# Three quotients of a fused attention and Mish kernel: from a logarithm and an exponential on ScalarE to a power of -1 on GpSimd

## The chip, the core and the metric

The kernel runs on one core of a Trainium2 chip. The core has five engines that run at the same time, each with its own queue of instructions that it works off in order: TensorE (PE in the profile; its weight loads are listed apart as PEld), VectorE (DVE), ScalarE (ACT), GpSimd (POOL) and SyncE (SP), which here only issues transfers. The metric is the device time of one execution in microseconds. Three runs of the kernel before took 1613.51, 1614.98 and 1616.91 us; the median is 1614.98 us.

## What is computed

The input x has 2048 rows of 512 numbers. Its normalized rows go two ways: through an attention of 32 heads of width 16 that share one key and one value head, and through two dense layers with a Mish activation between them. The output is x plus the product of the attention's result and a gate.

```python
xn = _layernorm(x)                                   # 2048 x 512
q = xn @ wq ; k = xn @ wk ; v = xn @ wv              # 32 heads of q, one of k and of v, width 16
p = _softmax(q k^T * 16 ** -0.5)                     # 32 x 2048 x 2048
s = (p @ v) @ wo                                     # 2048 x 512
h = xn @ w1 + b1                                     # 2048 x 1792
act = h * tanh(softplus(h))                          # Mish
y = act @ w2                                         # 2048 x 512
out = x + s * (y * sigmoid(y))
```

Three quotients are in it. With t = exp(h), tanh(softplus(h)) is t(t + 2) / (t(t + 2) + 2): the quotient of the first layer. The sigmoid of y is 1 / (1 + exp(-y)): the gate. And the attention divides each head's sum of p times v by the sum of its exponentials: the softmax.

## The kernel before, in words

All tiles have 128 partitions and, mostly, 512 columns of float32. The rows of x form four chunks of 512 (c = 0 to 3). Products that need full precision are made of three matmuls on numbers split into a high and a low part, so that most weights and activations exist as a pair of tiles ("high" by a copy to a rounded type, `hi_pool`; "low" by a subtraction, `sub`).

The work is written out by a Python program that decides the order of every instruction while it builds the kernel; the chip then only follows that order, with semaphores where one engine needs another's result. Order and waits are fixed; if an engine is later than the planner thought, the others wait for it.

- A **lead** of some 95 us normalizes x, makes keys and values and starts the first work. It has a planner of its own with a duration for each task; where TensorE has nothing to do it is given "warm" matmuls (L1178), whose results nobody reads.
- Then come 512 **steps** (the loop over `s`, L1286), 16 for each of 32 units of one head group. In a step TensorE makes four score tiles `e` (L875), ScalarE turns each into `pt` by an exponential (L877), and TensorE multiplies the `pt` of two steps ago by the values (`pv`, L949, the last matmuls of a step). TensorE also makes four tiles `m` (L895) for units to come; VectorE takes their row maxima (`mb`, L899), which give the shifts of the exponentials. `e` has three buffers in PSUM and `m` three.
- Between these matmuls lie the **dense matmuls** (`xps`), taken from a queue of groups of 12 or 15: the query groups (`q_group`), the first layer (`m1_group`, 14 per chunk, one for every 128 of the 1792 columns), the second layer (`m2_groups`, three thirds of 5, 5 and 4 first-layer tiles, four groups each) and the output projection (`wo_groups`). A group takes four steps: its matmuls are cut into chunks of 6 (or 8 and 7), and each chunk is done by halves of the partitions in two steps. A group is taken up only when the planner believes that its inputs are ready and the buffers that it will need free. If none is, the step has no dense matmuls. After step 490 no `m` are left, and a step has four dense matmuls over all partitions.
- What follows a group is a chain over other engines. **First layer** (`post` in `m1_group`, L647): ScalarE adds the bias (`hb`, L652); a "job" on ScalarE makes t = exp(hb) (L658); GpSimd limits it (L163), makes u = t + 2 (L661), u = u t and hb = hb u (L153); two more jobs on ScalarE make t = ln(u + 2) (L667) and t = exp(-t) (L671); then GpSimd multiplies hb by t and splits it into the pair `act` (L148, L153), which the second layer reads. **Gate** (L726 to L743): exp(-y) on ScalarE (L729), limited on GpSimd, ln(e + 1) and exp(-e) on ScalarE (L734, L739), y times e on GpSimd; four per chunk. **Softmax** (L972 to L990): once per 128 columns of heads, ln and exp(-) of the sums `sc` on ScalarE (L973, L977), then on GpSimd the product with `oc` and the split into `ot_all`, which the output projection reads.

Jobs are small pieces for ScalarE that wait in a list; `act_jobs` (L349) places one of them behind the exponentials of a step, two if more than two wait, and none in a step that had to move a result out of PSUM unless more than two wait. On GpSimd the planner keeps a clock: `charge(us)` (L133) adds the duration that it assumes for an operation (0.7 for one input, 1.3 for two), and `pool_at` (L143) gives the step at which the engine will be through, at 2.95 us per step. The first layer has three `hb` buffers, and the `t` tiles (which the gate shares) two.

The last unit's attention is finished by `o_last` (L1001), which has its own short form with a logarithm and an exponential; the change leaves it alone.

Of the kernel before, what the change touches and what calls it, by code (L numbers as in the profile page):

```python
# [14 lines left out]
F32 = mybir.dt.float32  # L15
F32R = mybir.dt.float32r
AF = mybir.ActivationFunctionType
ALU = mybir.AluOpType
AX = mybir.AxisListType

P = 128
# [26 lines left out]
NACT = 7  # L48
AHEAD = 2
THIRDS = ((0, 5), (5, 10), (10, 14))  # L50
TMAX = 2.0 ** 14
EMAX = 2.0 ** 60
TERMS = ((0, 0), (0, 1), (1, 0))
# [62 lines left out]
def block_kernel(ctx: ExitStack, tc: tile.TileContext, x, wq, wk, wv, wo, w1, b1, w2, out):  # L116
    nc = tc.nc
    cp = ctx.enter_context(tc.tile_pool(name="const", bufs=1))
# [8 lines left out]
    pe, act, dve, pool, sp = nc.tensor, nc.scalar, nc.vector, nc.gpsimd, nc.sync  # L127
# [5 lines left out]
    def charge(us):  # L133
        busy[0] = max(busy[0], step[0] * STEP_US + (0 if lead else 1.5)) + us
# [8 lines left out]
    def pool_at(margin):  # L143
        return max(math.ceil(2 * (busy[0] / STEP_US + margin)) / 2, step[0])
# [16 lines left out]
    def pool_min(o, lim):  # L161
        charge(0.7)
        pool.tensor_scalar(o, o, lim, 0.0, op0=ALU.min, op1=ALU.max)  # L163

    def f(ap):
        return ap.bitcast(F32)

# [1 line left out]
    dve.memset(f(qts[0]), 0.0)  # L169
    ident = cp.tile([P, P], F32, name="ident")  # L170
    make_identity(nc, ident)
    two = cp.tile([P, 1], F32, name="two")
    dve.memset(two, 2.0)
    one = cp.tile([P, 1], F32, name="one")
    dve.memset(one, 1.0)
    wk3 = sb.tile([P, 2, NDT, 64], F32R, tag="oc", name="wk3", bufs=1)
    wkf = sb.tile([P, NDT, 64], F32, tag="os", name="wkf", bufs=1)
    ks = cp.tile([P, S], F32R, name="ks")
# [144 lines left out]
    for j in range(4):  # L323
        o = slice(DH * j, DH * (j + 1))
# [6 lines left out]
    def at(s, fn):  # L331
        if s <= step[0]:
            fn()
        else:
            timed.setdefault(s, []).append(fn)

    def later(k, fn):
        at(step[0] + k, fn)
# [3 lines left out]
    def job(fn, free=None):  # L342

        jobs.append((fn, free))
# [299 lines left out]
    def m1_group(c, ft):  # L644
        it = item("ws", ("1", ft), w1[:, P * ft:P * (ft + 1)].rearrange("(t p) n -> p t n", p=P))

        def post(ps):  # L647
            hb = sb.tile([P, C], F32, tag="hb", name=f"hb{c}_{ft}", bufs=NHB)
            free_hb = hold(hb_hist)
            st = {}  # L650
            bias = b1c[:, ft:ft + 1]
            act.activation(hb, ps, AF.Identity, bias=bias)  # L652
            gap[0] += 1
            def st1():
                t = st["t"] = sb.tile([P, C], F32, tag="t", name=f"t{c}_{ft}", bufs=2)
                u = st["u"] = sb.tile([P, C], F32, tag="u", name=f"u{c}_{ft}", bufs=2)
                st["free"] = hold(t_hist)
                act.activation(t, hb, AF.Exp)  # L658
                pool_min(t, TMAX)
                charge(0.7)  # L660
                pool.tensor_scalar(u, t, 2.0, 1.0, op0=ALU.add, op1=ALU.mult)  # L661
                mul(pool, u, u, t)
                at(pool_at(0.3), lambda: job(st2))
                mul(pool, hb, hb, u)

            def st2():
                act.activation(st["t"], st["u"], AF.Ln, bias=two)  # L667
                job(st3)

            def st3():  # L670
                act.activation(st["t"], st["t"], AF.Exp, scale=-1.0)  # L671
                later(0.5, st4)

            job(st1, t_free)

            def st4():
                if extra(c, ft) == 0:
                    a = sb.tile([P, 2, C], F32R, tag="wq", name=f"act{c}_{ft}", bufs=1)
                elif extra(c, ft) == 1:
                    a = qts[(NU - 3) % 3]  # L680
                else:
                    a = sb.tile([P, 2, C], F32R, tag="act", name=f"act{c}_{ft}", bufs=NACT)
                act_of[c, ft] = a
                mul(pool, hb, hb, st["t"])
                st["free"]()
                hi_pool(a[:, 0], hb)
                sub(pool, a[:, 1], hb, f(a[:, 0]))
                m1_done[c, ft] = pool_at(0.2)
                free_hb()

        def slot():
            if extra(c, ft) >= 0:
                return 16 * (NU - 2) * extra(c, ft)
            return act_free[0] if act_live[0] < NACT else None

        def start():
            act_live[0] += extra(c, ft) < 0

        g = Group(mm12(lambda j, a: it.tile[:, a, P * j:P * (j + 1)],
                       lambda j, b_: xt_of[c][:, b_, j], NDT), post, [it],  # L700
                  [lambda: hb_hist[-NHB], slot, lambda: xt_done.get(c)], start=start)
        g.m1 = ft
        return g

    def m2_groups(c, third, its, m1s):
        lo, hi = THIRDS[third]

        def ready():
            return m1_done.get((c, hi - 1))

        def mk(tt):
            def post(ps):
                if tt == 3:
                    act_live[0] -= hi - lo
                if third == 0:
                    y_of[tt] = sb.tile([P, D], F32, tag=f"y{tt}", name=f"y{c}_{tt}", bufs=1)
                    act.activation(y_of[tt], ps, AF.Copy)
                    gap[0] += 1
                    return
                y = y_of[tt]  # L720
                dve.tensor_tensor(out=y, in0=ps, in1=y, op=ALU.add)  # L721
                if third < 2:
                    return
                st = {}

                def s1():  # L726
                    e = st["e"] = sb.tile([P, D], F32, tag="t", name=f"e{c}_{tt}", bufs=2)
                    st["free"] = hold(t_hist)
                    act.activation(e, y, AF.Exp, scale=-1.0)  # L729
                    pool_min(e, EMAX)  # L730
                    at(pool_at(0.3), lambda: job(s2))

                def s2():
                    act.activation(st["e"], st["e"], AF.Ln, bias=one)  # L734
                    job(s3)

                def s3():
                    e = st["e"]
                    act.activation(e, e, AF.Exp, scale=-1.0)  # L739
                    mul(pool, y, y, e)  # L740
                    y_done[c, tt] = pool_at(0.2)
                    st["free"]()
                later(0.5, lambda: job(s1, t_free))  # L743

            g = Group(mm12(lambda j, a: act_of[c, lo + j][:, a, P * tt:P * (tt + 1)],
                           lambda j, b: its[j].tile[:, b], hi - lo), post, its, [ready])
            g.dve = third > 0
            return g
        return [mk(tt) for tt in range(4)]
# [201 lines left out]
    def o_out(v):  # L951
        c, g = divmod(v, 8)
        b, k = divmod(g, 2)
        os_ = sb.tile([P, C], F32, tag="os", name=f"os{v}", bufs=1)
        if v == NU - 1:
            o_last(os_)
            return
        act.activation(os_, pv_of[v], AF.Copy)
        if k == 0:
            o_of[0] = sb.tile([P, C], F32, tag="oc", name=f"oc{v}", bufs=1)  # L960
            o_of[1] = sb.tile([P, C], F32, tag="sc", name=f"sc{v}", bufs=1)
        oc, sc = o_of[0], o_of[1]
        for e, t in ((16, sc), (0, oc)):
            for j in range(4):
                r = 64 * k + 16 * j
                sp_at(0.63)
                sp.dma_start(t[r:r + 16], os_[32 * j + e:32 * j + e + 16])
        rows = slice(0, HALF if v == NU - 2 else P)
        if v == NU - 2:
            turn_rows()  # L970
        if k == 1 or v == NU - 2:
            def n0():  # L972
                act.activation(sc[rows], sc[rows], AF.Ln)  # L973
                job(n1)

            def n1():
                act.activation(sc[rows], sc[rows], AF.Exp, scale=-1.0)  # L977
                later(0.5, n2)

            def n2():  # L980
                if b == 0 and c > 0 and wo_left[c - 1]:
                    later(0.5, n2)
                    return
                ot = ot_of[c, b] = ot_all[:, b]
                mul(pool, oc[rows], oc[rows], sc[rows])
                hi_pool(ot[rows, 0], oc[rows])
                sub(pool, ot[rows, 1], oc[rows], f(ot[rows, 0]))
                if k == 1:
                    ot_done[c, b] = pool_at(0.2)
            later(3, lambda: job(n0))  # L990

    turn_of = {}

# [120 lines left out]
    st = [task("DVE", 0.83, lambda t=t: stats(t), at=xat[t], prio=t // 4 * 2) for t in range(16)]  # L1114
    kv_done = None
    for c0, c1 in ((0, 1), (1, 2), (2, 4)):
# [4 lines left out]
        for c in range(c0, c1):  # L1121
            xs, his = [], []
            for t in range(4 * c, 4 * c + 4):
                sc = task(*(("ACT", 0.72), ("DVE", 0.4))[c == 0], lambda t=t: x_scale(t), [nrm])
# [72 lines left out]
    rows = []  # L1197
    cdone = [None]
    kind = [None]
    while True:  # L1200
# [21 lines left out]
        s, e, k = min(opts, key=lambda o: o[0])  # L1222
# [129 lines left out]
```

## Time and profile before

| | |
|---|---|
| runs, median (lowest to highest) | 1614.98 us (1613.51 to 1616.91) |
| span of the profiled execution | 1612.9 us |
| PE busy | 1594.2 us, 99% |
| DVE busy | 1348.5 us, 84% |
| ACT busy | 1294.7 us, 80% |
| POOL busy | 620.8 us, 38% |
| granted TensorE clock, mean | 0.999 |

The profile is of one execution. Its span runs from the first to the last instruction; the runs' times are of whole executions, and the one that was profiled has no time of its own beside the span. The span lies 2.1 us below the median of the runs, which is less than the 3.4 us between the lowest and the highest of them. A row of instructions gives line, engine, operation, what it writes and reads with the shape, and the count; then the busy time, the mean of one in ns, and the idle time of the engine just before these instructions, with what ended it. A row of a stretch gives its limits in us from the span's start, its length, then for each engine the busy time and the number of instructions, and at the end the granted clock and the transfers' share. A row of the waits gives who waited for whom, the total in us, how often, and the longest.

### The profile page before, as it was taken

What the parts mean: (1) busy time and instruction counts of PE and PEld (TensorE: products, weight loads), DVE (VectorE), ACT (ScalarE), POOL (GpSimd) and SP (SyncE); (2) the same over time, 40 slices, a digit from 0 to 9 for tenths busy, and PEclk for the clock granted to TensorE, in tenths of its full rate; (3) what the DMA queues carried; (4) which work ended last, traced back from release to release, by engine and by line L of the source; (5) the groups of instructions that cost most, each with busy time, mean ns of one, the idle gap of its engine ahead of it and who ended that gap; (6) DMA issues with size and microseconds to landing.
All of it is one profiled execution on the core that took longest, in us unless ns stands there. A gap on an engine that the chain in (4) does not pass through costs nothing.

```text
span 1612.9 us, 31471 instructions
## 1 busy us (share of the span) xinstructions
PE 1594.2 (99%) x11615; PEld 851.9 (53%) x11615; DVE 1348.5 (84%) x2300; ACT 1294.7 (80%) x2490; POOL 620.8 (38%) x627
## 2 busy tenths in 40 slices
PE   8999999999999999999999999999999999999998
PEld 5455545555555555555555555555555555555534
DVE  8988888888988888888898988888889898888802
ACT  5478788788888778877988787797788878879885
POOL 3875176166265103421524133154153223315522
PEclk9999999999999999999999999999999999999999
DMA  5332133042231304212113321231241313022020
GB/s 161 145 115 64 41 122 111 15 148 83 70 114 52 109 23 153 70 31 91 52 27 111 92 75 26 91 119 38 67 135 34 113 57 96 23 73 78 21 86 26
DMA packets 72776, 127.30 MB, mean 79 GB/s; under 512 B 21488, under 2 KB 34288, under 8 KB 72112
## 3 DMA queue, kind: packets, MB, share of 16 engines
q1 hardware_dynamic: 72624, 125.30, 24.9%
q8 instruction: 92, 1.51, 0.4%
q14 instruction: 60, 0.49, 0.1%
HBM read 76.36 MB, written 27.26 MB: 64 GB/s over the span
## 4 chain that ended last, share of the span: by engine, by line
PE 95%; DVE 2%; ACT 1%; DMA 1%; issue 0%; POOL 0%; SPq 0%; DVEq 0%; ACTq 0%; POOLq 0%
PE xps L109 46%; PE pv L949 31%; PE m L895 8%; PE e L875 5%; PE xps L105 3%; DVE mb L899 1%; PE wop L105 1%; PE warm L1178 0%; PE kp L289 0%; ACT xin L194 0%; DMA xin<-in_dram 0%; DVE st L214 0%; DMA ws<-w 0%; DVE xin L240 0%; PE xp L250 0%
## 5 line engine op out<-in xcount | busy, mean ns | idle before, releaser
L899 DVE TENSOR_REDUCE mb<-m 128x1 f32<-128x512 f32 x2048 | 1272.8, 683 | 184.4 <-PE m L895 157.5
L877 ACT ACTIVATE pt<-e 128x512 f32<-128x512 f32 x2048 | 1068.4, 604 | 253.0 <-PE e L875 236.8
L895 PE MATMUL m<-ks,qt 48*128 48x512 f32 (+1 forms) x2048 | 837.4, 422 | 3.0 <-DVE mb L899 2.5
L875 PE MATMUL e<-qt,ks 64*128 64x512 f32 x2048 | 746.4, 410 | 0.0
L949 PE MATMUL pv<-pt,vaug 128*32 128x512 f32 x4096 | 545.3, 605 | 0.0
L895 PEld LDWEIGHTS m<-ks,qt 48*128 48x128 f32 (+1 forms) x2048 | 370.6, 185 | 67.2 <-DVE mb L899 35.2
L875 PEld LDWEIGHTS e<-qt,ks 64*128 64x128 f32 x2048 | 370.7, 186 | 26.3 <-ACT pt L877 19.6
L109 PE MATMUL xps<-xt,ws 64*128 64x512 f32 x1248 | 345.8, 410 | 0.4 <-POOL ws L153 0.2
L109 PEld LDWEIGHTS xps<-xt,ws 64*128 64x128 f32 x1248 | 215.2, 185 | 205.9 <-ACT pt L877 135.2
L109 PE MATMUL xps<-wbs,act 64*128 64x512 f32 x1158 | 312.9, 407 | 0.1
L109 PEld LDWEIGHTS xps<-wbs,act 64*128 64x128 f32 x1158 | 201.9, 185 | 166.8 <-ACT pt L877 101.5
L949 PEld LDWEIGHTS pv<-pt,vaug 128*32 128x32 f32 x4096 | 80.7, 108 | 141.9 <-issue 133.2
L163 POOL TENSOR_SCALAR t<-t 128x512 f32<-128x512 f32 x56 | 34.5, 616 | 278.4 <-ACT t L658 278.4
L153 POOL TENSOR_TENSOR hb<-hb,t 128x512 f32<-128x512 f32 x56 | 72.3, 1292 | 152.4 <-PE m L895 74.0
L109 PE MATMUL xps<-xt,wq 64*128 64x512 f32 x336 | 93.0, 409 | 0.0
L109 PEld LDWEIGHTS xps<-xt,wq 64*128 64x128 f32 x336 | 58.0, 185 | 55.4 <-ACT pt L877 35.2
L109 PE MATMUL xps<-wbs,ot_all 64*128 64x512 f32 x288 | 79.3, 407 | 0.0
L109 PEld LDWEIGHTS xps<-wbs,ot_all 64*128 64x128 f32 x288 | 49.5, 184 | 47.2 <-ACT pt L877 30.2
L153 POOL TENSOR_TENSOR hb<-hb,u 128x512 f32<-128x512 f32 x56 | 72.3, 1291 | 4.4
L153 POOL TENSOR_TENSOR u<-u,t 128x512 f32<-128x512 f32 x56 | 71.9, 1284 | 4.7
L153 POOL TENSOR_TENSOR act<-hb,act 128x512 fp32r<-128x512 f32 x55 | 70.9, 1289 | 4.6
L721 DVE TENSOR_TENSOR y<-xps,y 128x512 f32<-128x512 f32 x32 | 21.9, 683 | 58.0 <-PE xps L105 58.0
(116 smaller groups left out, 826.7 us busy)
## 6 DMA issues: line engine op xcount, KB each, us to landing
ws<-w SPq DMA_DIRECT2D x38, 512.0 KB
wbs<-w SPq DMA_DIRECT2D x36, 512.0 KB
qt<-qh SPq DMA_DIRECT2D x256, 32.0 KB
w<-ws SPq DMA_DIRECT2D x14, 512.0 KB
w<-wbs SPq DMA_DIRECT2D x14, 512.0 KB
wq<-wq SPq DMA_DIRECT2D x13, 512.0 KB
wbs<-wo SPq DMA_DIRECT2D x12, 512.0 KB
rawwb<-in_dram SPq DMA_DIRECT2D x20, 256.0 KB
```

Of the source, the lines that this page charges most:

```text
L105: self.pe.matmul(ps, self.lhs(), self.rhs(), start=(self.k == 0), stop=(self.k == self.tot - 1))
L109: i = self.pe.matmul(ps, self.lhs()[o], self.rhs()[o], start=(self.k == 0 and self.halves == 0), stop=(self.k == self.tot - 1 and self.hal ...
L153: eng.tensor_tensor(out=o, in0=a, in1=b, op=op)
L163: pool.tensor_scalar(o, o, lim, 0.0, op0=ALU.min, op1=ALU.max)
L721: dve.tensor_tensor(out=y, in0=ps, in1=y, op=ALU.add)
L875: pe.matmul(e, ks[o:o + 64, P * k:P * (k + 1)], q[o:o + 64, p], start=True, stop=True)
L877: r = act.activation(pt, e, AF.Exp, scale=0.25)
L895: pe.matmul(m, q[o, p, P * t:P * (t + 1)], ks[o, C * kb:C * (kb + 1)], start=True, stop=True)
L899: return dve.reduce_max(out=mb_of[v][:, kb, z:z + 1], in_=m, axis=AX.X)
L949: pe.matmul(o[32 * j:32 * j + 32], vaug[:, k], pt, start=(k == 0), stop=(k == 15))
```

## The change

A new helper `inverse` raises a tile to the power of -1 on GpSimd, by an operation on two tiles whose second input is a column of -1 repeated along the row; if asked, it first adds a constant with an operation of its own. The planner is told 4.0 us for the power (`POW_US`). The first layer calls it with u + 2, the gate with e + 1, the softmax with `sc` alone. The logarithms and exponentials that did this on ScalarE go, and with them the jobs and the waits in planned steps between the engines: after the first exponential the rest of each chain is issued to GpSimd in one piece.

```diff
+POW_US = 4.0
...
+    def inverse(o, i, add=None):
+        if add is not None:
+            charge(0.7)
+            pool.tensor_scalar(i, i, add, 1.0, op0=ALU.add, op1=ALU.mult)
+        charge(POW_US)
+        pool.tensor_tensor(out=o, in0=i, in1=minus[0:i.shape[0]].to_broadcast(list(i.shape)), op=ALU.pow)
+
...
-    two = cp.tile([P, 1], F32, name="two")
-    dve.memset(two, 2.0)
-    one = cp.tile([P, 1], F32, name="one")
-    dve.memset(one, 1.0)
+    minus = cp.tile([P, 1], F32, name="minus")
+    dve.memset(minus, -1.0)
...
                 mul(pool, u, u, t)
-                at(pool_at(0.3), lambda: job(st2))
                 mul(pool, hb, hb, u)
-
-            def st2():
-                act.activation(st["t"], st["u"], AF.Ln, bias=two)
-                job(st3)
-
-            def st3():
-                act.activation(st["t"], st["t"], AF.Exp, scale=-1.0)
-                later(0.5, st4)
+                inverse(t, u, 2.0)
+                st4()
...
                     pool_min(e, EMAX)
-                    at(pool_at(0.3), lambda: job(s2))
-
-                def s2():
-                    act.activation(st["e"], st["e"], AF.Ln, bias=one)
-                    job(s3)
-
-                def s3():
-                    e = st["e"]
-                    act.activation(e, e, AF.Exp, scale=-1.0)
+                    inverse(e, e, 1.0)
                     mul(pool, y, y, e)
...
             def n0():
-                act.activation(sc[rows], sc[rows], AF.Ln)
-                job(n1)
-
-            def n1():
-                act.activation(sc[rows], sc[rows], AF.Exp, scale=-1.0)
-                later(0.5, n2)
+                inverse(sc[rows], sc[rows])
+                n2()
...
-            later(3, lambda: job(n0))
+            later(3, n0)
```

## The prediction

> **What bounds the kernel now.** I read the page's shares first, then the chain that ended last, then the waits, then stretches of the step loop.
>
> ```profile
> PE 1594.2 (99%) x11615; PEld 851.9 (53%) x11615; DVE 1348.5 (84%) x2300; ACT 1294.7 (80%) x2490; POOL 620.8 (38%) x627
> PE 95%; DVE 2%; ACT 1%; DMA 1%; issue 0%; POOL 0%; SPq 0%; DVEq 0%; ACTq 0%; POOLq 0%
> ```
>
> The second line is the chain by engine: TensorE carries 95% of it, ScalarE, which the change relieves, 1%, and GpSimd, which it loads, 0%. Who waits says the same:
>
> ```profile
> ACT pt L877 <- PE e L875: 236.8, 439, 1.1
> DVE mb L899 <- PE m L895: 157.5, 375, 1.2
> PEld e L875 <- ACT pt L877: 19.6, 33, 0.8
> ```
>
> ScalarE waits 236.8 us for scores and VectorE 157.5 us for `m`; the other way, score weights wait for an exponential 33 times, 19.6 us, and weight loads overlap matmuls. So ScalarE has slack in most steps already. Stretches of the loop show what sets a step:
>
> ```profile
> 901.56:936.45 34.89, 34.89 (x265) 18.96 (x264) 31.41 (x55) 25.28 (x51) 4.49 (x4) 1.00 0.30 91
> 1252.09:1275.27 23.18, 23.18 (x179) 12.53 (x177) 20.81 (x37) 19.93 (x39) 1.91 (x2) 1.00 0.35 114
> 446.67:469.66 22.99, 22.99 (x178) 12.39 (x177) 20.47 (x38) 20.87 (x42) 17.77 (x18) 1.00 0.28 98
> 224.25:232.37 8.12, 7.32 (x51) 2.68 (x49) 7.34 (x13) 6.83 (x15) 7.50 (x9) 1.00 0.50 163
> 232.37:235.52 3.15, 3.15 (x25) 1.51 (x23) 2.69 (x6) 2.77 (x6) 2.98 (x4) 1.00 0.98 349
> 58.00:82.00 24.00, 22.99 (x94) 12.48 (x93) 23.86 (x41) 8.49 (x15) 19.56 (x20) 1.00 0.36 122
> 96.89:1527.40 1430.51, 1427.52 (x10817) 767.40 (x10816) 1247.52 (x2106) 1185.59 (x2282) 536.28 (x538) 1.00 0.25 77
> ```
>
> The first three are whole steps with a dense chunk of 6: 12, 8 and 8 of them, so 2.908, 2.897 and 2.874 us each. ScalarE's count above four per step is its other work: 3, 7 and 10 instructions, and more of it makes no step longer. The fourth is three steps without dense matmuls, 2.71 us each; the fifth is the step behind them, 3.15 us. The sixth lies in the lead, where VectorE is full; the last is the loop while `m` lasts.
>
> **The change part by part.** Removed from ScalarE:
>
> ```profile
> L667 ACT ACTIVATE t<-u,two 128x512 f32<-128x512 f32 x56 | 41.6, 743 | 2.2 <-POOL u L153 2.2
> L671 ACT ACTIVATE t<-t 128x512 f32<-128x512 f32 x56 | 36.5, 651 | 0.1
> L734 ACT ACTIVATE e<-e,one 128x512 f32<-128x512 f32 x16 | 11.9, 742 | 0.8 <-POOL e L163 0.8
> L739 ACT ACTIVATE e<-e 128x512 f32<-128x512 f32 x16 | 10.4, 652 | 0.1
> L977 ACT ACTIVATE sc<-sc 128x512 f32<-128x512 f32 (+1 forms) x16 | 10.5, 659 | 0.0
> L973 ACT ACTIVATE sc<-sc 128x512 f32<-128x512 f32 (+1 forms) x16 | 10.4, 653 | 0.0
> ```
>
> These are 176 instructions and 121.3 us, 9% of ScalarE's busy time. Almost all lies beside TensorE. Directly it can give back no more than the 19.6 us of weight waits, and the matmuls behind them lost far less; nearest to zero, I take -1.5 us, bounds 0 and -20.
>
> Against it stands what the quiet steps show: the first stretch has 0.25 other ScalarE instructions a step, the second 0.9, and the step with fewer is 0.011 us longer, so 0.016 us per job, +2.9 us for 176. GpSimd's load works the other way: with about as many jobs a step, its busy share is 8% in the second stretch and 77% in the third, and the step is 0.023 us shorter, 0.03 us per full share. Nothing explains either, so I hold them for correlations. At 4 us a power GpSimd's share rises by a quarter (below): over the 364 six-matmul steps -3 us. I let the two cancel and keep ±3.
>
> Added to GpSimd: 88 powers (56, 16, 16), 72 additions (0.62 us by the row of L661 below), and by the order of the built kernel three high parts from ScalarE. The rows of a first-layer block:
>
> ```profile
> L163 POOL TENSOR_SCALAR t<-t 128x512 f32<-128x512 f32 x56 | 34.5, 616 | 278.4 <-ACT t L658 278.4
> L661 POOL TENSOR_SCALAR u<-t 128x512 f32<-128x512 f32 x56 | 34.8, 621 | 4.6
> L153 POOL TENSOR_TENSOR u<-u,t 128x512 f32<-128x512 f32 x56 | 71.9, 1284 | 4.7
> L153 POOL TENSOR_TENSOR hb<-hb,t 128x512 f32<-128x512 f32 x56 | 72.3, 1292 | 152.4 <-PE m L895 74.0
> L148 POOL TENSOR_SCALAR act<-hb 128x512 fp32r<-128x512 f32 x55 | 34.2, 622 | 4.8
> L153 POOL TENSOR_TENSOR xt<-xf,xt 128x1024 fp32r<-128x1024 f32 x2 | 4.8, 2382 | 3.0 <-ACT xt L274 3.0
> ```
>
> No row shows the power, P. Below it cannot be cheaper than a two-input operation of its size, 1.29 us. Above, no row bounds it; I take 8 us, six such passes, because a power needs a logarithm and an exponential. I take 4.0, the planner's charge, because the charges that have rows stand within 14% above them (0.7 for 0.62, 1.3 for 1.29, 2.5 for 2.38); likely P is 3.5 to 4.0. That this charge was measured too is my assumption.
>
> GpSimd's total at 4.0: 620.8 + 88 x 4.0 + 75 x 0.62 = 1019 us, 63%. The total fits; the question is local. A block has four operations of 0.62, four of 1.29 and the power; with some 0.07 us between starts (66.47 and 67.17 below for an operation of 0.62) it takes 8.3 + P, 12.3 us at 4.0. A first-layer group is four steps, 11.5 us. So GpSimd becomes the slower partner in runs of first-layer groups. The planner knows: it charges 12.0 per block and takes groups up accordingly, but at 2.95 us per step; at the measured 2.88 its 12.0 us pass in 11.7, so GpSimd falls behind by 0.6 us a block, 3 us over the five of a third. That is hidden, because the fourth and fifth tile of a third are read only two steps, 5.8 us, after its first group begins. Cost 0 at P = 4.0; with that cover gone the lateness lands on TensorE.
>
> In the built order the loop's steps without dense matmuls go from 12 in 9 places to 7 in 5, nearly all in the first chunk, and 18 dense matmuls leave the lead for the loop. Five filled steps cost 5 x (2.88 - 2.71) = +0.9; four fewer catch-up steps give 4 x (3.15 - 2.88) = -1.1. In the lead, warm matmuls replace the 18; VectorE is full there (23.86 of 24.00), so its end stays: 0, bounds ±1.
>
> SP's transfers keep their kind, and one is added; the query copies issued by SP stay at their planned steps, but their source on GpSimd comes later:
>
> ```profile
> 58.91 0.60 POOL L163 TENSOR_SCALAR t<-t 128x512 f32<-128x512 f32 x1
> ...
> 66.47 0.62 POOL L163 TENSOR_SCALAR t<-t 128x512 f32<-128x512 f32 x1
> 67.17 0.62 POOL L661 TENSOR_SCALAR u<-t 128x512 f32<-128x512 f32 x1
> ...
> 72.03 1.29 POOL L153 TENSOR_TENSOR ql<-qf,qh 128x512 fp32r<-128x512 f32 x1
> ```
>
> Two blocks with powers ahead of it put `ql`, done at 73.3, near 85 us; its copies are placed behind the loop's first steps, after 92 us. Behind them in SP's queue stand weight loads: 0 at P = 4.0.
>
> The end of the kernel, where the last two gates stand:
>
> ```profile
> 1589.05 0.65 ACT L729 ACTIVATE e<-y 128x512 f32<-128x512 f32 x1
> 1605.49 1.28 POOL L153 TENSOR_TENSOR xr<-xr,y 128x512 f32<-128x512 f32 x1 [5.64 <-DVE y L153]
> 1607.25 1.28 DVE L153 TENSOR_TENSOR y<-wop,y 128x512 f32<-128x512 f32 x2
> ```
>
> After 1589.70 GpSimd does two chains of limit, addition, power and product, 2 x (2.8 + P): at 4.0 until 1603.3. The next GpSimd work is due at 1605.49 and VectorE reads the last gate after 1607.25: hidden by 2.2 us, until P = 5.1, from where each us costs two.
>
> Sum against the span: -1.5 + 0 + 0.9 - 1.1 = -1.7, so 1611.2 us; the median of the runs lies 2.1 above the span, so 1613.3 us; I say 1613.5.
>
> **Rivals.** First, slower: the power takes longer than 4.0. Lateness per third is 5 x (8.3 + P - 11.7), against 5.8 us of cover, so it decides from P = 4.6, and in the first chunk, where weight splits fill GpSimd too, from about 4.2. With 12 thirds, P = 5 costs 12 x 2.2 = 26 us (1640), P = 5.5 some 56 (1670), P = 8 over 200. This is an upper count, since weight reloads and two blocks ahead soften it; I would halve it: 1627, 1642 and above 1715. For it: nothing measured shows P. Against: the charges' closeness to the rows.
>
> Second, faster: the step's dependence on GpSimd's share is real (-3 us), the one on jobs is not (0), and ScalarE's crowding costs a quarter of the 19.6 us of weight waits (-5). With the -0.2 of the empty steps that is 8.2 below the median, 1607 us. For it speaks the third stretch; against it that the first, with the least other work on ScalarE, is the slowest of the three.
>
> Third, a delay D at the first use of the power, in the lead. GpSimd's first block begins at 58.91; three blocks of 12.3, the query split and the weight split that the loop's first dense group needs (1.9 each) end near 99.6. It is read near 100.6, an empty step (2.7) and a step's `pv` (1.0) after 96.9. So the delay costs D - 1.0 once. The rows show no such gap before other first uses on GpSimd. For D = 3 it is +2, 1615 us. The Trainium skill's GPSIMD Engine Reference, section 2.1 "Instruction dispatch", says that the first call into freshly loaded GpSimd code pays about 6 us that no instruction shows; by that page, an estimate, it would be +5 us, 1618. No run here shows it for this operation.
>
> That the change does less than it says is no rival: the ScalarE instructions are gone from the built order.
>
> **Chances.** No change of weight, P at most 4.2: 0.52 (1609 to 1618; of it faster 0.14, same 0.26, slower 0.12). Power too slow: 0.30, slower. Faster rival: 0.14. First use: 0.04, same or slower by halves. About 0.2%, 3.2 us, is what a measurement of this kernel can tell. Together faster 0.28, same 0.28, slower 0.44. The range goes down to 1606 for the second rival and up to 1650, P near 6 by the halved count.
>
> **What would show it.** The power's row gives P: at most 4.2 for the forecast. ACT busy near 1175 us, POOL near 1020, ScalarE's wait for scores up, no new row of weight loads waiting for GpSimd's `act` or `ws`. Wrong if P is over 4.6, if ScalarE's exponentials wait for GpSimd to free `t` or `hb`, or if the last gate ends after 1605.

## The result: five times slower

The changed kernel takes 8076.66 us (median; 8074.56 to 8077.45), the kernel before 1614.6 us on the same chip: 5.0001 times as long, interval 4.9938 to 5.0064. The forecast was 1613.5 us with a range up to 1650. From the page of the kernel after, its first lines and the chain that ended last, by engine:

```profile
span 8072.6 us, 31665 instructions
PE 1782.0 (22%) x11639; PEld 920.5 (11%) x11639; DVE 1363.0 (17%) x2299; ACT 1207.6 (15%) x2311; POOL 7862.2 (97%) x784
POOL 60%; issue 5%; PE 1%; SPq 0%; DMA 0%; POOLq 0%; ACT 0%; DVE 0%; ACTq 0%
```

TensorE has gone from 99% of the span to 22%, and GpSimd from 38% to 97%; of the chain that ended last, GpSimd carries 60% of the span and TensorE 1%. One line of the kernel makes nearly all of GpSimd's time (groups of GpSimd, each shape by itself):

```profile
L171 POOL TENSOR_TENSOR t<-u,minus 128x512 f32<-128x512 f32 x56 | 4588.2, 81932 | 4.7
L171 POOL TENSOR_TENSOR e<-e,minus 128x512 f32<-128x512 f32 x16 | 1310.9, 81930 | 1.3
L171 POOL TENSOR_TENSOR sc<-sc,minus 128x512 f32<-128x512 f32 x15 | 1228.8, 81922 | 38.0 <-DMA sc<-os 38.0
L171 POOL TENSOR_TENSOR sc<-sc,minus 64x512 f32<-64x512 f32 x1 | 81.9, 81915 | 0.0
```

One power takes 81.93 us, not 4.0. The 88 of them take 4588.2 + 1310.9 + 1228.8 + 81.9 = 7209.8 us; GpSimd's other work is 7862.2 - 7209.8 = 652 us, and it stands idle for 210 us. These three make the span. Shared out over the powers, the loss is (8076.66 - 1614.6) / 88 = 73.4 us for each; if all of it is theirs, only 8.5 us of each is hidden.

The timeline of GpSimd around the first power (start, length, line) shows a whole block:

```profile
60.96 0.62 POOL L164 TENSOR_SCALAR t<-t 128x512 f32<-128x512 f32 x1
...
65.09 0.62 POOL L169 TENSOR_SCALAR u<-u 128x512 f32<-128x512 f32 x1
65.79 81.94 POOL L171 TENSOR_TENSOR t<-u,minus 128x512 f32<-128x512 f32 x1
147.81 1.26 POOL L154 TENSOR_TENSOR hb<-hb,t 128x512 f32<-128x512 f32 x1
...
151.10 0.62 POOL L164 TENSOR_SCALAR t<-t 128x512 f32<-128x512 f32 x1
```

From one block's first operation to the next it is 151.10 - 60.96 = 90.14 us, that is 8.2 + P: the prediction's block of 8.3 + P, with another P. How the other engines come to stand still is read from the waits (who for whom, total, times, longest):

```profile
DVE mb L890 <- PE m L886: 5625.4, 462, 174.9
PEld e L866 <- ACT pt L868: 3312.3, 58, 161.6
ACT t L664 <- POOL hb L154: 1921.9, 23, 162.3
PE m L886 <- DMA qt<-ql: 798.5, 10, 149.2
ACT e L728 <- POOL y L154: 741.1, 8, 156.4
PE xps L110 <- POOL ws L149: 621.3, 6, 174.3
```

Read from the cause upward: ScalarE's next job needs a `t` tile that GpSimd has not freed, 1921.9 us in 23 waits for the first layer and 741.1 in 8 for the gate, up to two powers at a time. Behind that job in ScalarE's queue stand the exponentials of the scores, so TensorE's score weights wait for `pt`, and VectorE waits for TensorE. The query's low parts and the weight splits, which stand in GpSimd's own queue behind powers, stop TensorE directly. The waits overlap and are not to be added up. Two stretches, one of the loop and one in it:

```profile
96.89:1527.40 1430.51, 341.40 (x2316) 176.23 (x2316) 272.61 (x453) 242.82 (x463) 1384.95 (x196) 0.61 0.06 21
98.00:156.00 58.00, 5.73 (x21) 3.23 (x25) 4.47 (x8) 6.89 (x13) 57.33 (x10) 0.50 0.00 0
```

In the time in which the kernel before did nearly its whole loop, TensorE worked 341 us, at a mean granted clock of 0.61; while it stands still behind a power, the clock is 0.50. The Trainium skill's "TensorE: Matmul & The Clock Gate", Part 1, says that the clock falls to half when TensorE has been idle for a window of some 3.4 us; the second row agrees.

At the end the last four gates run one behind another with nothing beside them (GpSimd's timeline):

```profile
7728.63 81.93 POOL L171 TENSOR_TENSOR e<-e,minus 128x512 f32<-128x512 f32 x1
7813.38 81.93 POOL L171 TENSOR_TENSOR e<-e,minus 128x512 f32<-128x512 f32 x1
7898.13 81.93 POOL L171 TENSOR_TENSOR e<-e,minus 128x512 f32<-128x512 f32 x1
7982.88 81.93 POOL L171 TENSOR_TENSOR e<-e,minus 128x512 f32<-128x512 f32 x1
```

### The profile page after: what moved, and what is told of

The parts are those of the page before. It is cut to its first block, busy times and chain, and to the rows that moved or that the text cites. A ratio compares the mean times of both kernels' runs of the same rounds, so it can differ in the third digit from the quotient of the medians.

```text
span 8072.6 us, 31665 instructions
## 1 busy us (share of the span) xinstructions
PE 1782.0 (22%) x11639; PEld 920.5 (11%) x11639; DVE 1363.0 (17%) x2299; ACT 1207.6 (15%) x2311; POOL 7862.2 (97%) x784
## 4 chain that ended last, share of the span: by engine, by line
POOL 60%; issue 5%; PE 1%; SPq 0%; DMA 0%; POOLq 0%; ACT 0%; DVE 0%; ACTq 0%
POOL t L171 37%; POOL e L171 12%; POOL sc L171 7%; POOL hb L154 1%; POOL u L154 1%; POOL act L154 0%; POOL u L169 0%; POOL u L667 0%; SPq L958 0%; POOL t L164 0%; POOL act L149 0%; PE xps L110 0%; PE pv L940 0%; POOL oc L154 0%; POOL ot_all L154 0%
## 5 line engine op out<-in xcount | busy, mean ns | idle before, releaser
L171 POOL TENSOR_TENSOR t<-u,minus 128x512 f32<-128x512 f32 x56 | 4588.2, 81932 | 4.7
L866 PE MATMUL e<-qt,ks 64*128 64x512 f32 x2048 | 812.9, 442 | 3849.7 <-ACT pt L868 3282.7
L171 POOL TENSOR_TENSOR sc<-sc,minus 128x512 f32<-128x512 f32 (+1 forms) x16 | 1310.8, 81922 | 38.0 <-DMA sc<-os 38.0
L171 POOL TENSOR_TENSOR e<-e,minus 128x512 f32<-128x512 f32 x16 | 1310.9, 81930 | 1.3
L886 PE MATMUL m<-ks,qt 48*128 48x512 f32 (+1 forms) x2048 | 897.3, 452 | 800.7 <-DMA qt<-ql 798.5
L866 PEld LDWEIGHTS e<-qt,ks 64*128 64x128 f32 x2048 | 409.9, 205 | 3898.8 <-ACT pt L868 3312.3
L110 PE MATMUL xps<-xt,ws 64*128 64x512 f32 x1272 | 393.8, 445 | 1017.1 <-POOL ws L149 621.3
L940 PE MATMUL pv<-pt,vaug 128*32 128x512 f32 x4096 | 599.3, 660 | 0.0
L886 PEld LDWEIGHTS m<-ks,qt 48*128 48x128 f32 (+1 forms) x2048 | 403.5, 201 | 867.5 <-issue 803.5
L664 ACT ACTIVATE t<-hb 128x512 f32<-128x512 f32 x56 | 36.0, 643 | 2291.9 <-POOL hb L154 1921.9
L728 ACT ACTIVATE e<-y 128x512 f32<-128x512 f32 x16 | 10.1, 632 | 1272.2 <-POOL y L154 741.1
```

The source lines that it names most:

```text
L110: i = self.pe.matmul(ps, self.lhs()[o], self.rhs()[o], start=(self.k == 0 and self.halves == 0), stop=(self.k == self.tot - 1 and self.hal ...
L171: pool.tensor_tensor(out=o, in0=i, in1=minus[0:i.shape[0]].to_broadcast(list(i.shape)), op=ALU.pow)
L866: pe.matmul(e, ks[o:o + 64, P * k:P * (k + 1)], q[o:o + 64, p], start=True, stop=True)
L886: pe.matmul(m, q[o, p, P * t:P * (t + 1)], ks[o, C * kb:C * (kb + 1)], start=True, stop=True)
L940: pe.matmul(o[32 * j:32 * j + 32], vaug[:, k], pt, start=(k == 0), stop=(k == 15))
```

## The experiments

The theory after the result: the length of the power on one in-order engine explains the loss, and nothing else in the change does. Rivals: the form of the operation (the repeated column, the tile's shape, the exponent) makes it slow; or the new order and the waits cost much by themselves. Beside these stood a smaller question: what would the change have done with the power at the price that the prediction took?

**The price by itself.** Six powers and one reciprocal are added behind the kernel before:

```diff
+    power(P, 512, pm.to_broadcast([P, 512]))
+    power(P, 256, pm.to_broadcast([P, 256]))
+    power(P, 64, pm.to_broadcast([P, 64]))
+    power(16, 512, pm[0:16].to_broadcast([16, 512]))
+    power(P, 512, p2)
+    power(P, 512, ph.to_broadcast([P, 512]))
+    dve.reciprocal(pd, p1)
```

Here `pm` is a column of -1 (`pminus` in the profile), `p2` a full tile of -1 (`pexp`) and `ph` a column of 2 (`phalf`).

> The kernel before, with six powers on GpSimd behind its last work, on a tile of 2.5: 512, 256 and 64 columns with a repeated column of -1; 512 columns on 16 partitions; 512 columns with a full tile of -1; 512 columns with an exponent of 2. They only lengthen the end. Theory: the power costs 0.160 us per column, whatever the partitions, the exponent and the way the second input is laid out: 82, 41, 10, 82, 82 and 82 us, and the span is 1613 + 379 = 1992 us. Rival 1, the repeated column is what is slow: the fifth takes 1.3 to 4 us and the span is near 1912 us. Rival 2, the exponent of -1 (a reciprocal) is slow: the sixth takes a few us.

Measured 1993.2 us against 1614.9. The groups:

```profile
L1353 POOL TENSOR_TENSOR pout<-pin,pexp 128x512 f32<-128x512 f32 x1 | 82.1, 82142 | 0.1
L1353 POOL TENSOR_TENSOR pout<-pin,pminus 128x512 f32<-128x512 f32 x1 | 81.9, 81948 | 1.7 <-DVE phalf L1350 1.7
L1353 POOL TENSOR_TENSOR pout<-pin,phalf 128x512 f32<-128x512 f32 x1 | 81.9, 81917 | 0.1
L1353 POOL TENSOR_TENSOR pout<-pin,pminus 16x512 f32<-16x512 f32 x1 | 81.9, 81905 | 0.1
L1353 POOL TENSOR_TENSOR pout<-pin,pminus 128x256 f32<-128x256 f32 x1 | 41.1, 41120 | 0.1
L1353 POOL TENSOR_TENSOR pout<-pin,pminus 128x64 f32<-128x64 f32 x1 | 10.5, 10515 | 0.1
L1360 DVE RECIPROCAL dout<-pin 128x512 f32<-128x512 f32 x1 | 3.3, 3343 | 0.0
```

The price goes by columns: (41.120 - 10.515) / 192 = 0.159 us per column and 0.3 us once. A full tile of exponents, an exponent of 2, or 16 rows in place of 128 change it by at most 0.3%. The rival of the form falls: no choice among these made the power cheap. An operation on one tile with the exponent as a constant was not run. The Trainium skill's "GPSIMD Engine Reference", section 2, says that each of GpSimd's eight cores has 16 partitions of its own; that 16 rows cost what 128 do agrees with it.

**One quotient at a time.** The kernel before with the power in the gate alone (the 16 quotients of L734 and L739 become `inverse(e, e, 1.0)`, as in the change), and with the power in the softmax alone (the 16 of L973 and L977).

> The kernel before with the power in the gate alone: 16 powers, the first layer and the softmax keep their logarithm and exponential. Theory (GpSimd works its queue in order, and everything behind a power waits for it, so that nearly the whole of each power shows): in the kernel after, each of 88 powers cost (8076.7 - 1614.6) / 88 = 73.4 us of the kernel's time; 16 x 73.4 = 1175, so 2790 us, and the last four gates alone, one behind another after the loop, cost 4 x 82 = 328 us. Rival (GpSimd stands idle for 62% of the kernel before, 992 us, and that absorbs most of the 16 x 81.9 = 1311 us that only four tiles per chunk wait for): GpSimd's total becomes 621 + 1311 + 10 = 1942 us and bounds the kernel, so at most some 1960 us.

> The kernel before with the power in the softmax alone: 16 powers, spread evenly, one every 32 steps (92 us). Theory (nearly the whole of each power shows, since the first layer's work stands behind it in GpSimd's queue and the shifts and products of the loop wait for that): 1615 + 16 x 73.4 = 2790 us. Rival (spread evenly, a power of 82 us fits into the idle 62% of its 92 us, less the 35 us that GpSimd works in it: 25 us late per power): 1615 + 16 x 25 = 2015 us, GpSimd nearly full.

Measured 2790.7 and 2622.1 us against 1616.8: 73.4 us per power of the gate, 62.8 per power of the softmax. The theory gave 2790 for both: the gate met it, the softmax came out 168 us below it. That the gate's 73.4 is also the mean over the 88 is in part luck, since four of its 16 powers run at the end with nothing beside them. GpSimd has 30% and 26% of the spans to spare, and still most of each power shows. Who waits, first in the run with the gate, then in the run with the softmax:

```profile
PEld e L877 <- ACT pt L879: 785.5, 42, 82.6
ACT e L739 <- POOL y L154: 555.2, 8, 84.1
```

```profile
PEld e L885 <- ACT pt L887: 859.0, 40, 75.5
ACT t L677 <- POOL u L154: 387.0, 13, 72.7
ACT t L668 <- POOL hb L154: 342.0, 6, 68.2
```

It is the chain read above. The softmax's powers, spread evenly over the loop, stop it too, because the first layer's products stand behind them in GpSimd's queue and ScalarE's queue waits for those. The rival, that spare time of the engine absorbs a long operation, falls in both.

**The same chain with a shorter quotient elsewhere.** The kernel after with VectorE's reciprocal; the additions stay on GpSimd:

```diff
-        pool.tensor_tensor(out=o, in0=i, in1=minus[0:i.shape[0]].to_broadcast(list(i.shape)), op=ALU.pow)
+        dve.reciprocal(o, i)
```

> The kernel after with VectorE's reciprocal in place of the power (88 of 3.34 us by the prices run, 294 us); the additions stay on GpSimd, the planner's charges as they were. Theory (it is the length of the one operation on GpSimd that costs the 6462 us, and nothing else of the change): the time falls back to within 300 us of the kernel before, at most 1615 + 294 = 1909 us; since VectorE works some 2.7 of each step's 2.9 us, most of a reciprocal should delay the row maxima and show: 1850 to 1900. Rival for the latter part (the m tiles run ahead of their use, and 8% of VectorE are idle): VectorE's sum of 1348 + 294 = 1642 us, so some 1660 us. Rival to the theory (something else in the chain, such as the wait of GpSimd in the middle of it, costs as much as the power): well above 2000 us.

Measured 2308.2 us against 1616.8. So 8076.7 - 2308.2 = 5768 us of the loss go with the power, but 691 us stay, 7.9 per quotient where the operation takes 3.35: both figures that I gave for this part were too low, and the time lies where the rival to the theory had it, well above 2000 us, though 691 is far from as much as the power costs. VectorE's groups show the rest:

```profile
L890 DVE TENSOR_REDUCE mb<-m 128x1 f32<-128x512 f32 x2048 | 1280.3, 682 | 287.9 <-PE m L886 253.6 <-PE xps L110 25.2 <-PE e L866 1.7
L171 DVE RECIPROCAL t<-u 128x512 f32<-128x512 f32 x56 | 187.8, 3353 | 293.4 <-POOL u L169 293.4
L171 DVE RECIPROCAL e<-e 128x512 f32<-128x512 f32 x16 | 53.6, 3353 | 36.2 <-POOL e L169 36.2
```

The reciprocals wait 293.4 + 36.2 = 330 us in VectorE's queue for GpSimd's additions, with the row maxima of the loop behind them; with their own 295 us that would be 625 of the 691, if all of it shows. So I was wrong to hold the operation's length for all of it. A quotient moved in one piece can also put a wait for another engine into its queue; on GpSimd that wait is not there, since the power follows GpSimd's own addition, and a stand-in of that length on GpSimd costs 7 us (next).

**What the predicted price would have done.** The kernel after with n multiplications in place of the power, n = 3, 6 and 1 (with 1, the planner is told 1.4). The quotients are left out. Each multiplication takes 1.04 us, so P is about 3.3, 6.6 and 1.0, less than the 4.1, 8.1 and 1.3 that the expectations took; a run at 4.0 there is not.

```diff
-        pool.tensor_tensor(out=o, in0=i, in1=minus[0:i.shape[0]].to_broadcast(list(i.shape)), op=ALU.pow)
+        for n in range(3):
+            pool.tensor_tensor(out=o, in0=(o if n else i), in1=(ones if n else minus)[0:i.shape[0]].to_broadcast(list(i.shape)), op=ALU.mult)
```

> The changed kernel with three multiplications by a repeated column (2 to the -60, then 1 twice) in the place of each power, about 4.1 us start to start, with the planner told 4.0 as in the change. It leaves the quotients out, so the activations, gates and attention outputs are scaled to almost nothing, but every engine has the same instructions otherwise. Theory, that of the prediction with only the price of the power wrong: 1613 us, between 1609 and 1618. Rival, GpSimd is late at 4 us already, or the moved work costs elsewhere: 1620 to 1640 us.

> As the one with three multiplications, but six, about 8.1 us, the planner still told 4.0; the quotients are left out here too. The prediction's count of late blocks, halved: over 1715 us, near 1720. Rival, the cover of 5.8 us per third is much larger than I took: below 1650 us.

> As before with one multiplication, 1.3 us, and the planner told 1.4: what a quotient on GpSimd could give if it cost no more than a product (the quotients are left out). Theory, ScalarE's 176 instructions are worth next to nothing off the critical path: 1612 us, within 4 of the kernel before. Rival, the faster rival of the prediction: 1607 us or less.

| operations in place of the power | P, us | time, us | ratio to before (interval) |
|---|---|---|---|
| 3 | 3.3 | 1622.0 | 1.0041 (1.0027 to 1.0054) |
| 6 | 6.6 | 1695.8 | 1.0498 (1.0481 to 1.0515) |
| 1 | 1.0 | 1623.3 | 1.0046 (1.0033 to 1.006) |

With P at 3.3 all else in the change, its order and its waits among it, costs 7 us: so some 6455 of the 6462 us lost go with the length of the power. At 6.6 the prediction's count of lateness gives 12 x (5 x (8.3 + 6.6 - 11.7) - 5.8) = 122 us, and 61 when halved; measured are 81. At 3.3 and at 1.0 the change would still have been 7 to 8 us slower, where the prediction had no change: with three the rival's 1620 to 1640 came, with six and with one neither of the two figures. In the run with three, two steps at 373 and 379 us took 6.09 and 4.15 us, 4.4 over two usual ones; in the second TensorE is busy throughout, at a granted clock of 0.68. The timelines of SP's queue, GpSimd and TensorE there:

```profile
371.14 2.29 SPq L450 DMA_DIRECT2D rawwb<-in_dram  x2
373.53 5.31 SPq L930 DMA_DIRECT2D qt<-cr  x8
...
371.78 1.29 POOL L154 TENSOR_TENSOR wbs<-rawwb,wbs 128x512 fp32r<-128x512 f32 x1
...
377.51 0.47 PE L869 MATMUL e<-qt,ks 64*128 64x512 f32 x1 [2.43 <-DMA qt<-cr]
```

A weight load in SP's queue went out only as GpSimd got through with the raw buffer, and the shifts for the next scores (`cr`) stood behind it. The run with one multiplication has such a stall too: a weight load goes out at 235.83, eight `cr` transfers follow at 236.25, TensorE waits 4.10 us for them, and the steps at 234 and 243 us take 8.69 and 4.00 us. So the stall is there at both prices. Of what else the run with three lost, 1.4 us lie in the lead (its loop begins at 98.25 us, not at 96.89), and the steps with six dense matmuls are longer, 2.896 us in place of 2.885 on average over those up to 2.96; the next runs are about these.

**Jobs on ScalarE and the length of a step.** Measured from the first `pv` of one step to that of the next, steps with six dense matmuls come mostly in two lengths, near 2.85 and near 2.91 us. Call those under 2.875 us short, and leave out those over 2.96. In the kernel before, 148 of 335 are short (44%): 31 of the 121 in which ScalarE does nothing but exponentials, 117 of the other 214. With three multiplications it is 97 of 344 (28%), with one 93 of 355. So the step without a job tends to be long. But the same count goes by GpSimd even more sharply: in the kernel before, 11 of the 126 steps in which GpSimd does nothing are short (4 of 65 without other work on ScalarE, 7 of 61 with it), and 137 of the 209 in which it works. Is it the missing instruction, ScalarE's lower load, what GpSimd does, or chance? Five runs looked into ScalarE's part; none of them changes GpSimd alone. First, the kernel before with a copy that nobody reads, in each step without a job:

```diff
+    spare = cp.tile([P, C // 2], F32, name="spare")
...
+            done = ran[0]
             act_jobs(1 + (len(jobs) > 2))
+            if ran[0] == done:
+                act.activation(spare, f(ks[:, 0:C // 2]), AF.Copy)
```

> The kernel before, with a copy of 128 x 256 on ScalarE (about 0.4 us, its result read by nobody) behind the exponentials of every step that has no job of ScalarE: 275 copies. Theory (the 0.016 us per job that the prediction read from quiet stretches, and held for chance, is real: a step gets shorter when ScalarE does more): 1614.6 - 275 x 0.016 = 1610.2 us. Rival (it was chance, or a job's place next to others): 1614.6 us, or some us slower where the copies delay an exponential. ACT busy rises by about 110 us in both.

Measured 1609.6 us, ratio 0.9958 (0.9946 to 0.9971), and ScalarE is busy 75 us more (1369.6). Second, the kernel before, in its own order, with each of the 176 logarithms and exponentials cut to 64 columns, as in

```diff
-                act.activation(st["t"], st["u"], AF.Ln, bias=two)
+                act.activation(st["t"][:, 0:64], st["u"][:, 0:64], AF.Ln, bias=two)
```

> The kernel before, in its own order on every engine, with each of the 176 logarithms and exponentials that the change removes cut to the first 64 of its 512 columns, some 0.25 us in place of 0.69: the rest of each quotient is left out, and the limits of t and e are set to 1 so that the numbers stay finite. ACT busy falls by about 77 us. Theory A (it is the new order of the work that makes even nearly free quotients on GpSimd 7 to 8 us slower, and relief of ScalarE alone is worth next to nothing): 1614.6 us, within 2. Theory B (a less busy ScalarE makes steps longer): if the 0.011 us per step between stretches goes by busy time, + 3 to 4 us, so 1618. Rival (relief of ScalarE takes away waits for exponentials): 1607 to 1612 us.

Measured 1612.1 us, ratio 0.9981 (0.9971 to 0.9991). ScalarE is 64 us less busy. That is 3 us better by the ratio, at the border between the figures that I gave for a gain and for none; steps are not longer (155 of 347 short), so theory B falls. Third, the copy cut to 128 x 16, 0.24 us. Fourth, the long copy in the stand-in of three multiplications.

> The kernel before with the copy cut to 128 x 16, some 0.2 us, in the same 275 places. Theory (it is the instruction between the last exponential of a step and the first of the next that turns a long step into a short one, whatever its length): as with the long copy, 1609.6 us, within 1.5. Rival (it is the time that ScalarE is busy, or how long it waits for the scores, that counts): near 1615 us, at least half of the 5.4 us lost.

> The stand-in of three multiplications (quotients left out as there), with ScalarE's copy of 128 x 256 behind the exponentials of every step that has no job: 426 copies. The stand-in was 7 us over the kernel before: by its trace 4.4 us in two steps stalled by a late transfer, 1.4 us in the lead, the rest in steps with six dense matmuls, which come in two lengths, 2.85 and 2.91 us, of which it had more long ones. Theory (a step without a job of ScalarE is mostly a long one, whatever the reason the jobs are gone): the copies win here what they won in the kernel before, 5 to 7 us, and some 2 more, so 1613 to 1615 us, with the two stalled steps still there. Rival (the copies helped only by their place in that order): 1619 to 1625 us.

Measured 1608.2 us (0.995; 0.9937 to 0.9962) and 1611.4 us (0.997; 0.9961 to 0.9979): the short copy does at least what the long one does, and the stand-in gains 10.6 us, more than the 7 to 9 expected, and passes the kernel before, with its two stalled steps still there. The same stretch of twelve quiet steps in four kernels: with three multiplications, the same with copies, before with narrow jobs, before with copies of 128 x 16 (each fence one kernel; the fourth pair of numbers is ScalarE's busy time and count):

```profile
908.08:942.95 34.87, 34.87 (x265) 19.14 (x264) 31.40 (x55) 25.27 (x51) 4.47 (x4) 1.00 0.20 62
```

```profile
901.68:935.97 34.29, 34.29 (x266) 18.40 (x264) 31.40 (x56) 28.86 (x63) 4.49 (x4) 1.00 0.21 65
```

```profile
902.14:937.02 34.88, 34.88 (x265) 19.04 (x264) 31.39 (x55) 25.27 (x51) 4.48 (x4) 1.00 0.29 93
```

```profile
898.48:932.81 34.33, 34.33 (x266) 18.45 (x264) 31.41 (x56) 26.47 (x63) 4.48 (x4) 1.00 0.31 92
```

The kernel before took 34.89 there. The same TensorE work takes 34.3 where ScalarE has a copy per step and 34.9 where it has none. The share of short steps is 77% with long copies, 78% with short ones, and 91% in the stand-in with copies. Last, the short copy also behind a job (`if ran[0] <= done + 1`), 482 copies:

> The run with copies of 128 x 16, now behind the job too in the steps that have one: 482 copies. Before it, 78% of the six-matmul steps were short ones of 2.85 us; of the long ones left, most hold a logarithm as their last ScalarE job, or a move out of PSUM. Theory (an instruction other than a logarithm between two steps' exponentials makes the step short): about 13% more of some 338 steps lose 0.05 us, 2 us, so 1606. Rival (it is enough that ScalarE does anything, and the further copies only delay the exponentials by 0.1 to 0.2 us where ScalarE is full): 1608 to 1612 us.

Measured 1605.5 us, ratio 0.9933 (0.9921 to 0.9945), 91% short: within half a us of what the theory gave, though the interval overlaps that of the run with 275 copies, so that the gain of the further copies is not shown beyond doubt by the time alone. It computes what the kernel before does, and it is faster than both kernels; it has nothing of the change in it.

## Why the prediction was wrong, point by point

**The power's price: the step that failed.** The prediction wrote "I take 4.0, the planner's charge, because the charges that have rows stand within 14% above them" and took 8 us, six passes of a two-input operation, as the upper end. The row says 81.93, 64 times the two-input row of 1.28. The three charges that stood near their rows were for operations that had been in the kernel; the fourth was for one that had not, and said nothing about it. The upper end had no more behind it, and the text said that no row bounds it. The lower end was no bound either: a multiplication by the repeated column takes 1.04 us, not 1.29. The price should have been left open at the top, with chance to match.

**The first rival named the mechanism.** The power too slow, deciding from P = 4.6, with a chance of 0.30: it is what happened, but its last figure was for P = 8. Its terms put to 81.9 give 12 x (5 x (8.3 + 81.9 - 11.7) - 5.8) = 4640 us for the first layer. If the two runs with one quotient may be added up, 8077 - 1617 - 16 x 73.4 - 16 x 62.8 = 4281 us are left for it: the full count, not the halved, is near for a long power. The gates and softmax were missing from that count.

**GpSimd's total** fitted at 4.0, and the prediction said that the question is local. The gate alone shows how local: GpSimd at 70% and 73.4 of 81.9 us visible.

**ScalarE's relief**, -1.5 us with bounds 0 and -20: the narrow jobs give -3.1, from 0.0019 x 1615, with over half of the jobs' time gone. The sign holds, and the size is within the bounds. ScalarE's busy time, for which the prediction had about 1175 us, is 1195.4 us with three multiplications: in the trace neighbours on ScalarE overlap by some 0.1 us, so that 121.3 us of rows free it for less.

**The two correlations that were left to cancel.** "+0.016 us per job" removed has something real in it: 275 short copies take 0.005 x 1615 = 8.1 us off, 0.029 per copy, 7.6 us of it in the 359 steps with six dense matmuls. That a job of the kernel's own does what a copy does isn't shown: where GpSimd does nothing, the steps with other work on ScalarE are nearly all long too (54 of 61). "-0.03 us per full share" of GpSimd did not come between kernels: with the same jobs, the stand-ins with one and with three multiplications (GpSimd at 46% and 58%) have the same mean step, 2.896 us over those up to 2.96. Within each kernel without copies it holds in another form, by whether GpSimd works in a step at all: 4 of 79 against 93 of 265 short with three multiplications, 4 of 124 against 89 of 231 with one. The prediction had the first at +2.9, saw no reason for it, and struck it out against the second; why either holds stays open.

**SP's queue**, "0 at P = 4.0": 4.4 us at P = 3.3, and 6.9 in two steps at P = 1.0. It considered the query's copies; what came late were the shifts, behind a weight load waiting for its raw buffer. Together with the steps this makes the forecast case wrong by 7 to 8 us at the two prices below its own that were run; at 4.0 itself, between 3.3 (+7) and 6.6 (+81), the change would most likely have been slower too, on the side to which it gave 0.44.

**The tail**, hidden until P = 5.1, each us beyond costing two: four gates stand there in place of two, 84.7 us apart.

**First use.** The third rival's delay is not there: the first power starts 0.08 us behind the addition ahead of it and takes 81.94, like the rest. The Trainium skill's "GPSIMD Engine Reference", section 2.1 "Instruction dispatch", has about 6 us for a first call into freshly loaded code; no run here shows it for this operation.

**Said beforehand to show an error:** a power row over 4.6, exponentials that wait for GpSimd to free `t`, a last gate after 1605. All three came.

## What to carry to other kernels

An operation that the kernel has never run has no price until it has been run alone; a number in the source, a planner's charge above all, is not a row, and a range has to stay open where nothing bounds it. On an engine that works in order, one long operation shows for the most part (62.8 and 73.4 of 81.9 us here), however idle the engine is otherwise, as soon as another engine's queue waits for something behind it. One instruction more on an engine that is not the bound can make the bound's steps shorter; that relieving such an engine makes them longer isn't shown, since no run took the jobs away in the order of the kernel before. A small regularity between stretches of the trace, here 0.01 us a step, is worth a run when the step comes hundreds of times.

## What the runs showed of the hardware that was not expected

- GpSimd's power takes 0.159 us per column plus 0.3, 81.9 us for 128 x 512, whatever the rows (16 to 128), the exponent (-1 or 2) and the layout of the exponents. VectorE's reciprocal takes 3.34 us for the same tile, 2.4 times the 1.39 that ScalarE's logarithm and exponential take together.
- A ScalarE instruction of 0.24 us between the exponentials of two steps makes a step with six dense matmuls 0.05 us shorter (34.33 for 34.89 us over twelve). In the kernel before, steps with just their four exponentials on ScalarE have the same gaps and lengths among these to 2 ns, but for ScalarE's one wait for scores: median 0.788 us in the short ones and 0.843 in the long. Why the instruction ahead matters stays open. Not any will do: in the kernel before, of 9 steps that held only the first layer's logarithm and in which GpSimd stood idle, 2 were short; of 28 that held only its second exponential 25 were, but GpSimd worked in all of these. Where GpSimd stands idle 4 of 65 steps with exponentials alone were short, where it works 27 of 56; with copies of 128 x 16 it is 53 of 66 and 39 of 57. What GpSimd's work does at the time these runs don't separate.
- While TensorE stood behind a power the granted clock was 0.50, and it was 0.602 over the whole changed kernel. TensorE's busy time is 1782 us, 188 more than before, and a score matmul takes 442 ns on average in place of 410; that the clock is the cause of it was not tested.
